# A new written order for the instructions of a fused attention and feed-forward kernel

## The chip, the cores and the metric

The kernel runs on one core of a Trainium2 chip. Its time is the device time of one execution in microseconds (us); three runs gave 105.85, 105.78 and 106.14, median 105.85. A core has TensorE (PE, matrix products, with the loading of their weights shown apart as PEld), VectorE (DVE), ScalarE (ACT), GpSimd (POOL) and SyncE (SP). SP here only issues DMAs; ACT issues a few as well. Each of them takes its instructions strictly in the order in which the program gives them, so an instruction that waits holds up all that are behind it on the same engine, DMA issues included.

## The reference

There are 4 batches and 4 heads, 1088 positions and 32 values a head. First comes an attention without softmax. `a` and `b` are 8 sketches each of q or of k, and their 64 products are the features:

```python
    def phi(x):
        a = np.einsum('rd,bhsd->bhsr', S1, x)
        b = np.einsum('rd,bhsd->bhsr', S2, x)
        return np.einsum('bhsi,bhsj->bhsij', a, b).reshape(*x.shape[:-1], r * r)
    q_p, k_p = (phi(q), phi(k))
    kv = np.einsum('bhsf,bhsd->bhfd', k_p, v)
    z = np.sum(k_p, axis=2)
    num = np.einsum('bhsf,bhfd->bhsd', q_p, kv)
    den = np.einsum('bhsf,bhf->bhs', q_p, z)[..., None] + 1e-06
```

num / den, with the heads side by side, is the 128-wide input x of a feed-forward block:

```python
    mu = np.mean(x, axis=-1, keepdims=True)
    var = np.mean((x - mu) ** 2, axis=-1, keepdims=True)
    xn = (x - mu) / np.sqrt(var + 1e-06) * g_ln
    ch = np.maximum(xn @ w_ch1, 0.0) @ w_ch2
    return (x + ch).astype(np.float32)
```

w_ch1 is 128 x 512 and w_ch2 is 512 x 128. S1, S2, w_ch1 and w_ch2 come as 64-bit floats; everything else is 32-bit.

## The kernel before

The kernel is one long list of small named steps, the text `PROGRAM`. A loop reads it from front to back and calls the function of each name; the order of the names is the order of the instructions on every engine, and dependencies between tiles become waits. Nothing reorders it. A step names its batch, its part, and where one is given its engine (S for SP, A for ACT, G for POOL, V for DVE) and its PSUM bank (X, Y, M, N, O or K).

The steps, in the order in which one batch needs them:

- Loads: `ld`, `ld_u` (k and q), `ld_vh`, `ld_v`, `ld_vr` (v), `ld_w` (the two weights), `ld_s`. `gate` is a one-column memset by POOL in the tile that a load will fill, so that the load, and every DMA behind it on SP, waits until POOL has come to that place.
- The sketch matrix: `w_bits`, `w_ex`, `w_exf`, `w_mant`, `w_e2`, `w_addlow`, `w_e3` and `s_heads` make a 32-bit S from the 64-bit words; `sk` and `sk_s` are products that turn it; `sk_0`, `sk_2`, `sk_8`, `sk_d`, `sk_q`, `sk_qq` arrange it. The two weights go the same way with `w_low`, `w_exn`, `w_en`, `w_add`, `w_mul` (the first one in two halves, columns 0 to 256 and 256 to 512); `fold` puts the layer norm's scale and centring into the first, and `fold_cp` copies it out of PSUM.
- k: `turn_u`, `turn_g`, `turn_r` transpose (DVE), `k_dir` or `k_feat` are the sketch products, `k_cp` or `k_tok` take them out of PSUM, `k_prod` forms the features (POOL, in batch 0 partly DVE as `k_prod0`), `k_sum`, `k_zs`, `k_sc`, `k_sccp` make the normaliser, `k_val` is features times v. From batch 1 on its result goes through DRAM (`k_turn`, `k_wr`, `k_rd`); in batch 0 it stays on the chip (`k_vcp`, `k_spr`, `k_rcp`).
- q: the same with `q_dir`, `q_c`, `q_dirw`, `q_ctok`, `q_cpw`, `q_ac0`, `q_den`, `q_rec`, `q_b0`, `q_prod0`, `q_turn` in batch 0, and `q_feat`, `q_tok`, `q_ac`, `q_den`, `q_rec`, `q_a2`, `q_prod`, `q_turn` later. `num` is the product of the turned q features with the k result and `num_cp` its copy: a batch gives two chunks of 512 columns (chunks 2b and 2b+1), and the remaining 64 positions of two batches form the small chunks 8 and 9.
- The feed-forward block by chunk: `hid` (one of 4 groups of 128 hidden rows, columns in quarters t0 to t1) and `relu` out of PSUM; `sec` (4 accumulating products for one quarter of the columns); `row_turn`, `row_wr`, `row_rd` bring the chunk into rows through DRAM; `st_bn`, `st_ag`, `st_pow` make the layer norm's factor; `fin` joins the parts and `store` writes out.

`fill` and `tick` compute nothing that is used: products of a tile of ones, which keep TensorE at work; `fill 8 64 O` is 8 products 64 columns wide into bank O, and `tick` is a 4-column product on a 32 x 32 corner. Every 32-bit product is carried out as two passes, so a count of 18 in the trace is 9 products.

The lines of the profile that the prediction uses: L275 is `fill`, L280 `tick`, L408 `sk`, L412 `sk_s`, L416 `sk_0`, L423 `sk_2`, L466 `turn_u`, L509 `k_dir` and `q_dir`, L556 `k_sum`, L588 `k_val`, L654 `q_ctok`, L740 `q_turn`, L756 `num`, L858 `hid`, L874 `sec`, L887 `fin`, L107 `gate`, L174 the load of the second weight, L80 ACT's copies.

Three places set the order of the work around the change. Batch 0 has nothing before it: its steps wait for loads and for each other, with DVE nearly full. From about 20 us `hid` and `sec` of one batch are laid between the attention products of the next. And in the last 20 us only `hid`, `sec`, `fin` and stores of the last chunks are left.

## Time and profile before

| | |
|---|---|
| median of 3 runs | 105.85 us |
| profiled execution, and its span | 105.92 us, 104.2 us |
| first and last TensorE product, start and end | 1.44 us, 100.45 us |
| TensorE idle from 8.48 to 43.63 us | 2.12 us |
| TensorE idle from 43.63 to 100.45 us | 0.02 us |
| first load of k landed, first load of q landed | 4.6 us, 7.1 us |
| DVE busy from 8.48 to 24.00 us | 14.00 of 15.52 us |
| POOL busy from 24.00 to 43.63 us | 16.53 of 19.63 us |

Times within the trace count from the start of the span. The span is 1.72 us shorter than the execution's own time. An engine's share of the whole span says little here: which engine ends a wait last is read for each stage.

### The profile page before, as it was taken

Reading aid. Unit: us, or ns where it says so; the run is one execution under the profiler, and the core shown is the slowest. Engines: PE = TensorE matmul, PEld = TensorE weight load, DVE = VectorE, ACT = ScalarE, POOL = GpSimd, SP = SyncE. Lnnn points to the kernel's source line nnn. Section 1 sums busy time; section 2 is a strip of 40 time slices with the busy share of each in tenths; the row PEclk is TensorE's granted clock in tenths of the full one; section 3 lists DMA queues with packets and bytes.
Section 4 is the critical chain, followed back from the end, with each engine's and each line's share of the span. In section 5 each row is a group of like instructions: output and inputs, shape, how many; then the busy total and the mean of one; then the engine's idle time right before and its main releaser. Section 6 shows DMA issues by size and latency. Waiting matters only on the chain.

```text
span 104.2 us, 3418 instructions
## 1 busy us (share of the span) xinstructions
PE 96.9 (93%) x1369; PEld 72.2 (69%) x1369; DVE 74.1 (71%) x233; ACT 36.4 (35%) x90; POOL 50.2 (48%) x69
## 2 busy tenths in 40 slices
PE   4999987999999879999999999999999999999950
PEld 4999976785545679863249779573498864499940
DVE  5619589999989599377999849986957660265530
ACT  0400628369384100053635052206620427730300
POOL 6400582543795999740299992314990300021500
PEclk9999999999999999999999999999999999999999
DMA  1898800399589467524624443423344165440442
GB/s 21 241 307 216 266 15 3 118 352 298 153 271 243 97 165 231 168 79 136 205 65 142 128 105 107 144 84 89 89 120 132 50 227 140 139 131 6 104 124 56
DMA packets 17744, 15.01 MB, mean 144 GB/s; under 512 B 5568, under 2 KB 14656, under 8 KB 17728
## 3 DMA queue, kind: packets, MB, share of 16 engines
q1 hardware_dynamic: 16240, 13.90, 45.5%
q10 hardware_dynamic: 1456, 0.89, 3.3%
q8 instruction: 11, 0.18, 0.8%
q14 instruction: 5, 0.04, 0.1%
q0 software_dynamic: 32, 0.00, 0.0%
HBM read 10.29 MB, written 4.49 MB: 142 GB/s over the span
## 4 chain that ended last, share of the span: by engine, by line
PE 92%; ACT 2%; issue 1%; DVE 1%; DVEq 0%
PE M L858 21%; PE M L874 20%; PE PO L858 9%; PE PO L874 7%; PE X L756 7%; PE PO L275 6%; PE KV L588 4%; PE X L509 3%; PE X L693 2%; PE PO L280 2%; PE X L532 2%; PE X L874 2%; PE KV L556 1%; PE KV L874 1%; PE M L509 1%
## 5 line engine op out<-in xcount | busy, mean ns | idle before, releaser
L847 POOL TENSOR_TENSOR rstd<-va,mhalf 128x4 f32<-128x4 f32 (+1 forms) x10 | 9.2, 922 | 29.5 <-DVE va L841 29.4
L874 PE MATMUL M<-w,hT 128*128 128x128 f32 x184 | 23.0, 277 | 0.0
L874 PEld LDWEIGHTS M<-w,hT 128*128 128x128 f32 x184 | 21.8, 192 | 1.6 <-ACT hT L866 0.8
L858 PE MATMUL M<-xT,w 128*128 128x512 f32 (+1 forms) x50 | 22.7, 564 | 0.0
L866 ACT ACTIVATE hT<-M 128x512 f32<-128x512 f32 (+2 forms) x29 | 14.7, 509 | 19.3 <-PE M L858 17.8
L85 POOL TENSOR_TENSOR kp<-kf 128x1024 f32<-128x1024 f32 (+3 forms) x8 | 15.0, 1890 | 1.2 <-DVE kf L541 0.6
L858 PEld LDWEIGHTS M<-xT,w 128*128 128x128 f32 x50 | 8.2, 189 | 9.0 <-issue 5.2
L85 POOL TENSOR_TENSOR qp<-a,fq 128x1280 f32<-128x1280 f32 (+1 forms) x6 | 13.0, 2175 | 0.2
L740 DVE STREAM_TRANSPOSE qpT<-qp 128x1280 f32<-128x1280 f32 (+2 forms) x9 | 11.0, 1228 | 1.6 <-POOL qp L85 1.5
L80 ACT COPY xT<-X 128x256 f32<-128x256 f32 (+1 forms) x18 | 5.6, 362 | 17.5 <-PE X L756 17.5
L866 ACT ACTIVATE hT<-PO 128x512 f32<-128x512 f32 (+2 forms) x15 | 7.3, 484 | 12.0 <-PE PO L858 11.9
L858 PE MATMUL PO<-xT,w 128*128 128x512 f32 (+1 forms) x22 | 10.6, 561 | 0.0
L834 DVE BATCH_NORM_STATS2 st<-x 128x6 f32<-128x128 f32 x32 | 6.9, 278 | 3.4 <-DMA x<-xd 2.9
L874 PE MATMUL PO<-w,hT 128*128 128x128 f32 x64 | 8.1, 278 | 0.9 <-issue 0.9
L874 PEld LDWEIGHTS PO<-w,hT 128*128 128x128 f32 x64 | 7.7, 192 | 1.8 <-issue 1.8
L756 PE MATMUL X<-qpT,kvr 32*32 32x288 f32 (+2 forms) x384 | 7.7, 332 | 0.9 <-ACT low L335 0.9
L887 DVE SCALAR_TENSOR_TENSOR ob<-M,rstd,x 128x128 f32<-128x128 f32 x21 | 6.2, 335 | 2.2 <-issue 1.1
L817 DVE STREAM_TRANSPOSE xh<-xT 128x512 f32<-128x512 f32 x8 | 5.6, 698 | 2.4 <-ACT xT L80 2.4
L756 PEld LDWEIGHTS X<-qpT,kvr 32*32 32x32 f32 x384 | 4.6, 103 | 2.9 <-ACT low L335 1.1
L275 PE MATMUL PO<-ones 128*128 128x64 f32 (+2 forms) x24 | 6.4, 430 | 0.0
L358 POOL TENSOR_TENSOR mant<-mant,low 128x256 f32<-128x256 f32 (+1 forms) x3 | 3.0, 1002 | 5.4 <-ACT mant L327 3.0
L858 PEld LDWEIGHTS PO<-xT,w 128*128 128x128 f32 x22 | 3.8, 190 | 2.4 <-issue 1.9
(132 smaller groups left out, 134.7 us busy)
## 6 DMA issues: line engine op xcount, KB each, us to landing
xd<-xh SPq DMA_DIRECT2D x8, 256.0 KB, 2.1
x<-xd SPq DMA_DIRECT2D x32, 64.0 KB, 2.0
vn<-in_v_dram SPq DMA_DIRECT2D x13, 128.0 KB, 4.1
kn<-in_k_dram SPq DMA_DIRECT2D x3, 544.0 KB, 6.0
qn<-in_q_dram SPq DMA_DIRECT2D x3, 544.0 KB, 4.5
out_dram<-ob SPq DMA_DIRECT2D x24, 64.0 KB, 1.7
qn<-in_q_dram SPq DMA_DIRECT2D x2, 256.0 KB, 4.3
w_raw<-in_moe_w_ch_dram SPq DMA_DIRECT2D x2, 256.0 KB, 4.7
```

Source lines behind the costliest of these rows:

```text
L80: act.copy(o, i)
L85: by[eng].tensor_tensor(out=o, in0=a, in1=b, op=ALU.mult)
L275: pe.matmul(banks[z][:, 0:w], ones[:, 0:P], ones[:, 0:w], start=True, stop=True)
L740: dve.transpose(_ap(qpT, 0, P, 32 * u0, [[32, u1 - u0], [TW, 8], [1, 32]]), qp[:, H * F * u0 : H * F * u1])
L756: pe.matmul(XS[r // 2][D * h : D * h + D, o : o + w], kvr[b % 2][rows, fs * f + hs * h : fs * f + hs * h + D], qpT[rows, c : c + w], start ...
L817: dve.transpose(_ap(xh[c % 2], 0, P, 0, [[32, n], [D * n, 4], [1, 32]]), cols(c))
L834: dve.bn_stats(out=sts[slot(c)][:, 6 * t : 6 * t + 6], in_=row_ap(c, t))
L847: pool.tensor_tensor(out=rstds[slot(c)][:, 0:n], in0=vas[slot(c)][:, 0:n], in1=mhalf[:, 0:n], op=ALU.pow)
L858: pe.matmul(banks[z][:, 0:n], w1[:, P * j : P * (j + 1)], cols(c)[:, a : a + n], start=True, stop=True)
L866: act.activation(o, i, AF.Relu)
L874: pe.matmul(banks[z][:, DM * t : DM * (t + 1)], h[:, 512 * j + P * t : 512 * j + P * (t + 1)], w2[:, DM * j : DM * (j + 1)], start=(j == 0 ...
L887: dve.scalar_tensor_tensor(out=o, in0=i0, scalar=rstds[slot(c)][:, t : t + 1], in1=row_ap(c, t), op0=ALU.mult, op1=ALU.add)
```

## The change

The list `PROGRAM` is replaced; no function changes. All steps that compute something stay, and the sizes of the products stay; what differs:

- The products of ones. Before: 12 and 5 small ones (`tick`), 8 of 64 columns, one of 256 behind `sk`, one of 128 behind `k_sum`, and two of 256 between the first `num` and the first `fold`. After: one of 512 and one of 368 columns ahead of `sk`, then 128 and 240 ahead of `q_c`, 240 and 256 ahead of the first `fold`, 272 behind the first `num`, 160 ahead of the first `hid`.
- Gates. Before: the second weight and k of batch 2. After: k of batch 1, the second weight, and q of batch 1.
- The orders of all engines, from the start (`c_m8`, `c_m32`, `c_m2` and the POOL memsets change places; `sk_s` comes before `k_dir`) to the end (which chunk's group goes to which bank, and when; `c_act`, a one-element activation, becomes the last step).

```diff
@@ -922,92 +922,91 @@
     PROGRAM = """
-    ld_s S 0; c_ones; ld_s A 1; c_iota; ld_u S k 0 0 4; ld_u A k 0 4 8; ld_g; c_m8; tick 12 O;
-    ld_u S q 0 0 4; ld A k 0 32 34; c_m32; fill 8 64 O; ld_w S 1 0 256; c_vpad 1; ld_vr A 0 32;
-    c_sf; w_bits V 0 0 32; w_ex V 0 0 32; ld_vh S 0; c_ident; w_exf V 0 0 32; ld_vr A 0 33;
-    c_small; w_mant V 0 0 32; w_e2 V 0 0 32; w_addlow V 0 0 32; w_e3 V 0 0 32; c_rest; s_heads V;
-    tick 5 O; c_pads 0; ld_vh S 1; sk; turn_u k 0 0 4; c_ac 0; fill 1 256 O; ld_vh S 2; sk_0;
-    turn_u k 0 4 8; k_dir 0 4 X; ld_vh S 3; turn_r k 0; c_m2; ld_u S q 0 4 8; ld S q 0 32 34;
-    w_ex V 1 0 256; w_bits V 1 0 256; k_dir 4 9 Y; turn_u q 0 0 4; ld_w S 1 256 512; k_cp A 0 4 X;
-    sk_q; w_mant A 1 0 256; ld S k 1 0 34; k_prod0 0 3 X 0; sk_8; c_cg G; k_prod G 0 3 4; sk_s;
-    k_cp A 4 9 Y; q_dir 0 4 M; sk_2; w_exn A 1 0 256; k_prod0 4 6 Y 4; k_prod G 0 6 9;
-    w_en A 1 0 256; k_sum 0; fill 1 128 O; k_zs 0; k_sc 0; w_e3 V 1 0 256; sk_qq 2; k_sccp A 0;
-    c_pads 1; turn_u q 0 4 8; q_c 0 4 X; c_vpad 0; sk_d; k_val 0; q_ctok 0 4 X; k_scd G;
-    q_ac0 0 4 M 0 0; turn_r q 0; q_den 0 0 4; w_ex V 1 256 512; q_dirw 4 9 N; q_rec 0 0 4;
-    k_vcp A 0; w_bits V 1 256 512; q_b0 0 4 M 0 0; w_exn A 1 256 512; q_prod0 0 2 M 0 0;
-    w_low A 1 0 256; w_mant A 1 256 512; k_spr 0; w_add G 1 0 256; q_turn 0 2; q_cpw A 4 9 N;
-    k_rcp A 0; q_ac0 4 9 N 4 1; w_low A 1 256 512; gate w 2; num 0 0 2; ld_w S 2 0 512;
-    q_prod0 2 4 M 0 0; w_add G 1 256 512; ld S q 1 0 34; q_den 0 4 9; fill 1 256 O; q_turn 2 4;
-    num_cp A 0 1 0 2; w_mul G 1 0 256; w_en A 1 256 512; fill 1 256 O; q_rec 0 4 9;
-    num_cp A 0 0 0 2; q_b0 4 9 N 4 1; fold O 0 256; w_e3 V 1 256 512; q_prod0 4 9 N 4 1;
-    num 0 2 4; w_mul G 1 256 512; fold_cp A O 0 256; hid M 0 0 0 2; gate k 2; c_vpad 3;
-    ld S k 2 0 34; num_cp A 0 1 2 4; c_ac 1; c_vpad 2; turn_r k 1; fold O 256 512; ld_v S 1 0;
-    sk_qq 3; q_turn 4 9; relu A M 0 0 0 2; hid N 0 1 0 2; num_cp A 0 0 2 4; ld_v S 1 1;
-    fold_cp A O 256 512; hid M 0 0 2 4; w_low A 2 0 512; ld_v S 1 2; hid O 0 2 0 2;
-    relu A M 0 0 2 4; w_bits V 2 0 512; num 0 4 9; relu A N 0 1 0 2; turn_g k 1 0 4;
-    relu A O 0 2 0 2; w_mant A 2 0 512; hid N 0 1 2 4; w_ex V 2 0 512; num_cp A 0 0 4 8;
-    num_r A 0; w_add G 2 0 512; num_cp A 0 1 4 8; k_feat 1; relu A N 0 1 2 4; row_turn 1;
-    hid M 1 1 0 4; k_tok 1; row_wr S 1; ld_v S 1 3; turn_g q 1 0 4; hid O 0 3 0 2; k_prod G 1 5 9;
-    ld_vr S 1 33; k_sum 1; relu A O 0 3 0 2; hid N 0 3 2 4; ld S q 2 0 34; w_exn A 2 0 512;
-    k_zs 1; k_sc 1; hid O 1 2 0 4; relu A N 0 3 2 4; k_sccp V 1; turn_r q 1; w_en A 2 0 512;
...
-    store S 4 0; row_rd S 7 1; sec M 6 0; st_bn 6; store S 5 2; store_r S 8 3; sec M 6 1; st_ag 6;
-    relu A N 9 1 0 1; relu A O 7 0 0 4; store_r S 8 0; st_pow 6; sec M 6 3; st_bn 7; sec M 6 2;
-    sec K 7 3; fin M 6 0; fin M 6 2; fin M 6 1; hid O 9 2 0 1; st_ag 7; sec Y 7 1;
-    relu A O 9 2 0 1; store A 4 3; fin M 6 3; st_pow 7; store S 6 0; store A 5 1; hid N 9 0 0 1;
-    sec M 7 2; store S 6 2; relu A N 9 0 0 1; st_pow 9; fin K 7 3; hid O 9 3 0 1; sec X 7 0;
-    fin M 7 2; relu A O 9 3 0 1; fin Y 7 1; store A 6 1; store A 6 3; sec N 9 0; fin X 7 0;
-    store S 7 2; store A 7 3; store S 7 0; store A 7 1; fin N 9 0; store_r S 9 0; store_r A 9 1;
-    store_r S 9 2; store_r A 9 3;
+    ld_s S 0; c_ones; ld_s A 1; c_iota; ld_u S k 0 0 4; ld_u A k 0 4 8; ld_g; c_m32; fill 1 512 O;
+    ld_u S q 0 0 4; ld A k 0 32 34; c_m2; ld_w S 1 0 256; c_vpad 1; ld_vr A 0 32; c_pads 0;
+    w_bits V 0 0 32; ld_vh S 0; c_small; c_ac 0; ld_vr A 0 33; w_ex V 0 0 32; w_mant V 0 0 32;
+    c_sf; w_exf V 0 0 32; c_ident; w_e2 V 0 0 32; w_addlow V 0 0 32; fill 1 368 O; w_e3 V 0 0 32;
+    c_m8; c_vpad 2; s_heads V; ld_vh S 1; c_rest; turn_u k 0 0 4; sk; ld_vh S 2; sk_q; sk_0;
+    turn_u k 0 4 8; sk_s; k_dir 0 4 X; ld_vh S 3; c_cg G; turn_r k 0; sk_d; turn_u q 0 0 4;
+    ld_u S q 0 4 8; k_dir 4 9 Y; k_cp A 0 4 X; ld S q 0 32 34; w_bits V 1 0 256; w_low A 1 0 256;
+    k_prod G 0 3 4; k_prod0 0 3 X 0; ld_w S 1 256 512; q_dir 0 4 M; k_cp A 4 9 Y; w_ex V 1 0 256;
+    sk_2; k_prod G 0 6 9; w_exn A 1 0 256; k_prod0 4 6 Y 4; k_sum 0; w_en A 1 0 256; k_zs 0;
+    k_sc 0; w_mant A 1 0 256; fill 1 128 O; k_sccp A 0; fill 1 240 O; c_pads 1; w_e3 V 1 0 256;
+    turn_u q 0 4 8; c_vpad 0; q_c 0 4 X; k_scd G; k_val 0; gate k 1; c_ac 1; ld S k 1 0 34;
+    q_ctok 0 4 X; w_add G 1 0 256; turn_r q 0; q_ac0 0 4 M 0 0; q_den 0 0 4; q_dirw 4 9 N;
+    w_ex V 1 256 512; k_vcp A 0; q_rec 0 0 4; w_low A 1 256 512; q_b0 0 4 M 0 0;
+    w_bits V 1 256 512; q_prod0 0 2 M 0 0; k_spr 0; q_prod0 2 4 M 0 0; fill 1 240 O;
+    q_cpw A 4 9 N; w_exn A 1 256 512; gate w 2; w_mul G 1 0 256; fill 1 256 O; ld_w S 2 0 512;
+    q_ac0 4 9 N 4 1; w_mant A 1 256 512; q_turn 0 2; w_en A 1 256 512; w_add G 1 256 512;
+    fold O 0 256; k_rcp A 0; q_den 0 4 9; q_rec 0 4 9; num 0 0 2; w_e3 V 1 256 512;
+    q_b0 4 9 N 4 1; w_mul G 1 256 512; q_turn 2 4; fill 1 272 M; num_cp A 0 1 0 2;
+    fold_cp A O 0 256; q_prod0 4 9 N 4 1; fold M 256 512; num_cp A 0 0 0 2; fill 1 160 O;
+    fold_cp A M 256 512; hid O 0 1 0 2; gate q 1; sk_8; num 0 2 4; ld S q 1 0 34; q_turn 4 9;
+    w_low A 2 0 512; ld S k 2 0 34; hid M 0 2 0 2; ld_v S 1 0; num_cp A 0 1 2 4; num_cp A 0 0 2 4;
+    hid N 0 3 0 2; ld_v S 1 1; w_bits V 2 0 512; num 0 4 9; ld_v S 1 2; w_ex V 2 0 512;
+    relu A N 0 3 0 2; turn_r k 1; relu A O 0 1 0 2; ld_v S 1 3; turn_g k 1 0 4; w_mant A 2 0 512;
+    hid N 0 3 2 4; num_cp A 0 0 4 8; w_add G 2 0 512; num_r A 0; hid O 0 0 2 4; num_cp A 0 1 4 8;
+    relu A N 0 3 2 4; k_feat 1; row_turn 1; relu A M 0 2 0 2; relu A O 0 0 2 4; hid M 0 0 0 2;
+    row_wr S 1; k_tok 1; hid O 0 1 2 4; ld_vr S 1 33; relu A M 0 0 0 2; turn_g q 1 0 4;
+    k_prod G 1 5 9; k_sum 1; ld S q 2 0 34; hid N 1 2 0 4; k_zs 1; turn_r q 1; turn_r k 2; k_sc 1;
+    hid M 0 2 2 4; k_sccp V 1; turn_g k 2 0 4; q_feat 1; k_prod G 1 0 5; relu A M 0 2 2 4;
+    relu A N 1 2 0 4; hid M 1 0 0 4; w_exn A 2 0 512; q_tok 1 1; q_tok 1 0; hid N 1 3 0 4;
+    w_en A 2 0 512; relu A O 0 1 2 4; sk_qq 2; w_e3 V 2 0 512; k_val 1; relu A N 1 3 0 4;
+    row_rd S 1 1; q_ac V 1 4 9; q_ac V 1 0 4; ld S k 3 0 34; w_mul G 2 0 512; q_den 1 4 9;
...
+    relu A N 7 0 0 4; row_rd S 6 2; st_bn 9; hid O 9 1 0 1; st_ag 9; row_rd S 7 3;
+    relu A M 7 2 0 4; sec N 6 0; row_rd S 7 1; row_rd S 7 0; hid M 9 0 0 1; relu A O 9 1 0 1;
+    sec N 6 2; relu A M 9 0 0 1; row_rd S 7 2; store A 5 1; store_r S 8 2; sec N 6 1; store S 2 2;
+    hid O 9 2 0 1; store S 4 2; st_bn 6; hid M 7 1 0 4; relu A O 9 2 0 1; store A 5 3; sec N 6 3;
+    st_ag 6; relu A M 7 1 0 4; st_bn 7; st_pow 6; sec Y 7 1; st_ag 7; sec X 7 0; fin N 6 2;
+    st_pow 9; fin N 6 0; sec M 7 2; st_pow 7; fin N 6 1; fin N 6 3; store S 6 0; store A 6 1;
+    hid O 9 3 0 1; fin X 7 0; sec K 7 3; store S 6 2; relu A O 9 3 0 1; fin Y 7 1; store A 4 1;
+    fin M 7 2; store A 6 3; sec N 9 0; fin K 7 3; store S 7 0; store A 7 3; store A 7 1;
+    store S 7 2; fin N 9 0; store_r A 9 3; store_r S 9 0; store_r S 9 2; store_r A 9 1; c_act;
     """
```

## The prediction

> **What bounds the kernel now.** First the page's first two parts: how full each engine is, and where.

> ```profile
> span 104.2 us, 3418 instructions
> PE 96.9 (93%) x1369; PEld 72.2 (69%) x1369; DVE 74.1 (71%) x233; ACT 36.4 (35%) x90; POOL 50.2 (48%) x69
> ...
> PE   4999987999999879999999999999999999999950
> ...
> DVE  5619589999989599377999849986957660265530
> ```

> TensorE is full nearly everywhere, so the end is its start plus its work plus its pauses. Which part of that work is useful shows in the chain that ended last, in order of time (start, length, what):

> ```profile
> 1.44 1.44 PE PO L280 x24
> 2.88 3.60 PE PO L275 x16
> 6.48 0.62 PE PO L280 x10
> 7.11 0.72 PE KV L408 x2
> 7.83 0.85 PE PO L275 x2
> 8.68 3.53 PE X L509 x18
> ...
> 36.14 0.92 issue
> ...
> 99.54 0.91 PE M L874 x8
> ```

> The reader is to see that sk (L408) starts at 7.11 behind 5.7 us of products of ones, and that the 18 passes of k_dir (L509) take 196 ns each. Third, the instructions in order of time, DVE's of the start:

> ```profile
> 3.63 0.28 DVE L85 TENSOR_TENSOR s_f<-mant,bits 16x128 f32<-16x128 f32 x1
> 4.61 1.09 DVE L466 STREAM_TRANSPOSE kT<-kn 128x512 f32<-128x512 f32 x1 [0.70 <-DMA kn<-in_k_dram]
> 7.87 0.23 DVE L416 TENSOR_TENSOR sk<-KV,m 128x64 f32<-128x64 f32 x1 [2.16 <-PE KV L408]
> 10.83 0.96 DVE L85 TENSOR_TENSOR kp<-X,kf 128x768 f32<-128x768 f32 x1 [0.38 <-ACT kf L80]
> 12.47 0.29 DVE L423 TENSOR_TENSOR s2b<-KV,m 128x128 f32<-128x128 f32 x1 [0.69 <-PE KV L412]
> 13.68 0.19 DVE L564 TENSOR_TENSOR zT<-KV,m 128x32 f32<-128x32 f32 x1 [0.28 <-PE KV L556]
> 15.10 0.32 DVE L654 STREAM_TRANSPOSE qc<-X 128x128 f32<-128x128 f32 x1
> 22.38 1.47 DVE L740 STREAM_TRANSPOSE qpT<-qp 128x1280 f32<-128x1280 f32 x1
> ```

> sk's operand (the first row) is ready at 3.91; DVE loses 2.16 us to sk all the same. From there to 24 us DVE is busy 14.00 of 15.52 us: it sets the pace of batch 0. From 43.63 to 100.45 TensorE never pauses. Fourth, products by group, 11.0 to 11.5 us and then 12.3 to 13.4 us:

> ```profile
> L509 PE MATMUL X<-sk,kT 128*128 128x128 f32 x5 | 1.3, 420 | 0.0
> ```
> ```profile
> L509 PE MATMUL M<-sk,qT 128*128 128x128 f32 x8 | 1.1, 275 | 0.0
> ```

> The same product takes 420 ns, then 275: TensorE runs at half rate until about 11.7 us, though the granted clock reads 1.00 throughout.

> **The change, part by part.** The sum is made against the profiled execution, 105.92 us (span 104.2, 1.72 around it); the median is 0.07 lower.

> *Products of ones at the start.* 12 + 5 small ones and 8 of 64 columns go. At half rate a 128-column pass takes 0.196 us, so 512 and 368 columns, two passes each, take 2 x (4.0 + 2.88) x 0.196 = 2.7 us: from 1.44 to 4.1, some 0.2 later with the first weights. Then sk can start at about 4.4: c_m8 (0.10 and 0.16) now stands ahead of s_heads, which then ends near 4.3. sk takes 0.72, so sk_0 waits only for turn_u, which no order can start before k's landing at 4.6: it runs at 5.70, not 7.87. That is 2.17 us. k_dir follows at 6.0 (before 8.48).

> *DVE up to q_ctok.* The waits of 0.38, 0.69 and 0.28 us in the rows above go: k_cp and sk_s are earlier, and k_sum is ready when k_zs comes. c_m2, 0.25 by the spacing of its rows, moves ahead of k's landing, into DVE's 0.70 of waiting. Next late are the loads, whose issues up to the first weight's second half stand in the old order: q at 7.1 (0.2 us of waiting at turn_u), then w_e3, held by ACT's conversions (0.1), and q_ctok behind the longer fill (128 + 240 columns, 0.77 us against 0.27; about 0.25 of it shows). So 2.17 + 1.35 + 0.25 - 0.55 = 3.2; I take 3.1, q_ctok at 12.0. This has k_dir at full rate, 18 x 0.111 (q_dir's 0.89 over 8). At half rate the second k_cp comes 1.3 us later and k_prod0 4 6 0.7: 2.4 instead of 3.1. Which, depends on whether 2.7 us of wide products and sk wake TensorE where 9 us of narrow ones did not before 11.7. I take full rate, because from 7 us on the products were wide and the change came 4.7 us later; both ends stay in the range. [...]

> *q_ctok to the last q_turn.* 8.75 us before; the same instructions, without turn_r k 1 (0.22), which comes right behind. So q_turn 4 9 ends at 20.75, not 23.85, and 2.9 of lead stays on DVE. The fills here: 240 + 256 columns (1.03 by the 0.53 of a 256-column one) lie between k_spr, done at 14.7, and the first num, which waits for k_rcp behind three conversions on ACT (0.5 each) until 16.4: hidden, with 0.1 to spare. 272 columns (0.56) lie in the wait for w_mul's second half; 160 (0.33) in the wait of num 0 4 9 for q_turn. Without these covers they would cost their 2.2 us; the two removed fills of 256 (1.06) lay beside DVE work as well.

> *TensorE at num 0 4 9.* It starts at 20.8, not 23.91, but three half-width hid products lie behind it, not four: 0.45 of the 3.1 is owed. The lead is 2.65.

> *Loads and gates.* Issues take 0.4 to 0.5 each on SP. k of batch 1 (544 KB, ungated at 8.77 before) now waits for a gate behind k_scd, about 11.5, and the second weight for one behind w_add, 12.4 (before 18.10). Both move where the DMA share was 0.02 (13.33 to 18.47). At the 300 GB/s of the busy slices 1.06 MB take 3.5 us: landed near 16.5, first read at 20.8. Behind gate q 1 (POOL, after the second w_mul, 17.9) SP holds q 1, k 2 and v of batch 1, 1.65 MB: 5.5 us and 2 of latency, 25.4. turn_g q 1 wants q at 24.8, which comes first (about 22); k_val 1 wants v at 29.4. Hidden; if the transfers ran at the 200 GB/s of 24 to 43 us, v would come at 28.2 and still be in time.

> *POOL.* The memsets change places while POOL waits; sk_qq 2 (0.39) moves into its full stretch, ahead of w_mul. k_prod 2 then ends near 41.3, before 43.66, and k_val 2 starts near 42: hidden.

> *From batch 1 on.* The same products in a new order. Before, TensorE's pauses from 24 to 100 were 0.92 us at 36.14, with no releaser shown. I leave it in (0 to 0.92 to gain). New waits: hid M 2 3 comes 4.3 us after num 1's start and needs bank M, which fin 1 frees; before, st_bn 1 to the last fin took 3.86 and began 0.2 behind num's start, so 0.2 us of room. Likewise hid N 6 1 behind fin 4, room 0.25, and the last k_rd 3, ten issues behind the stores that follow k_wr 3, room 1.5. I take 0.2 of loss, with 0 and 1.5 as ends (all three rooms missed by one slow issue of 1.6, as k_rd at 38.24 was). c_act (0.2) stands behind ACT's last issue, while stores still land: nothing. The end, one sec, one fin and four small stores, is as before: 3.75 us.

> Sum: 105.92 - 2.65 + 0.2 = 103.47; less 0.07 for the median, 103.4.

> **Rivals.**

> 1. *The lead is given back in part.* k_dir stays at half rate (0.7), and the three rooms are missed (1.3): 103.4 + 0.7 + 0.6 to 1.3, about 104.9. For it: POOL is busy 16.53 of 19.63 us up to num 1. Against it: the pauses after 24 us were 0.92 in all.
> 2. *The head was not the bound.* If batch 1 waits for a load or POOL anyway, all is given back and it stays at 105.9. Against it: loads of batch 1 have free DMA time, and POOL's k_prod 1 starts from k_tok, which moves with DVE.
> 3. *TensorE falls back to half rate, and it is slower.* Place: from k_dir to the first num the new order has pauses (about 1 us between k_sum and k_sc). The work there, fills included, is 8.6 us at full rate, by the rows; at half rate 17.2, and the first num would start at 23.2 instead of 16.4, the lead of 2.65 turned into a loss of 3.2 with the fold and fills that lay behind it before: 109. Up to 2.65 us of lost time it is not slower, so it decides once the half rate lasts over some 5.3 us of products. Against it: pauses of 0.28 and 0.93 us from 13.3 to 18.5 (TensorE busy 3.94 of 5.14) brought none before. [...]

> **Numbers.** Forecast 0.58, own range 102.5 to 104.3; rival 1 0.15; rival 2 0.07; slower 0.20, half of it rival 3 (107 to 109) and half waits in the new order beyond the ends above, just over 106. The lowest end is the lead of 3.1 with the 0.92 gone: 101.9. Runs here differ by 0.3%, so changes below that count as none. Faster 0.73, same 0.07, slower 0.20; range 102.2 to 106.4, which leaves out some 0.05 below and 0.13 above.

> **What would show it.** sk_0 at 5.7 to 6.0; k_dir's passes at 275 ns; q_ctok at 12.0; num 0 4 9 at 20.8; TensorE without pauses of over 0.3 us from there but the one near 33 to 36, and its last product ending near 97.9. It is wrong if L509 stays at 420 ns, if hid or num wait for loads, or if TensorE pauses after 40 us.

## The result and the profile after

The changed kernel takes 104.85 us in the median of 20 executions (102.09 to 108.39); the kernel before, on the same occasions, took 106.75 in the median of 20 (105.17 to 109.38). One kernel's executions differ by up to 6%, so the ratio is formed from those within 1.5% of each kernel's fastest (4 of the changed kernel's, 10 of before's): 0.967, with a 95% interval of 0.961 to 0.973. The medians of all executions alone would give 0.982. Forecast were 103.4 us against 105.85, a ratio of 0.977.

The profiled execution of the changed kernel took 104.31 us (span 102.5, 1.81 around it). Its page, first two parts:

```profile
span 102.5 us, 3333 instructions
PE 95.9 (94%) x1327; PEld 69.1 (67%) x1327; DVE 73.3 (71%) x233; ACT 36.6 (36%) x90; POOL 50.0 (49%) x70
...
PE   4979898999999999999999999999999999999950
...
DVE  4995589997998789369975996679459790237720
```

TensorE's row has no gap left in its middle: the 0.92 us at 36.14 of before is gone. The last product ends at 98.77 (before 100.45), and from there to the end of the span it is 3.7 us in both, so all of the gain lies ahead of the last product. DVE's rows of the start, from the instructions in order of time (start, length, what; in brackets the wait and what ended it):

```profile
4.11 0.27 DVE L85 TENSOR_TENSOR s_f<-mant,bits 16x128 f32<-16x128 f32 x1
4.54 1.08 DVE L466 STREAM_TRANSPOSE kT<-kn 128x512 f32<-128x512 f32 x1 [0.16 <-DMA kn<-in_k_dram]
5.54 0.23 DVE L416 TENSOR_TENSOR sk<-KV,m 128x64 f32<-128x64 f32 x1
8.82 0.96 DVE L85 TENSOR_TENSOR kp<-X,kf 128x768 f32<-128x768 f32 x1 [1.07 <-ACT kf L80]
11.01 0.69 DVE L85 TENSOR_TENSOR kp<-X,kf 128x512 f32<-128x512 f32 x1 [0.83 <-ACT kf L80]
12.09 0.19 DVE L564 TENSOR_TENSOR zT<-KV,m 128x32 f32<-128x32 f32 x1 [0.39 <-PE KV L556]
13.88 0.32 DVE L654 STREAM_TRANSPOSE qc<-X 128x128 f32<-128x128 f32 x1 [0.41 <-PE X L646]
20.86 1.51 DVE L740 STREAM_TRANSPOSE qpT<-qp 128x1280 f32<-128x1280 f32 x1
```

sk_0 (L416) runs at 5.54 and no longer waits: 2.33 us earlier than before. But the waits for ACT's copies (L80) have grown to 1.07 and 0.83, and q_ctok (L654) comes at 13.88, only 1.22 earlier. TensorE's products show why; the first block is from its instructions in order of time from 5 to 7 us, those in the second block its groups from 5.5 to 11 us (busy, mean ns of one, idle before):

```profile
5.91 0.77 PE L412 MATMUL KV<-s_f,ident 128*128 128x128 f32 x2 [0.61 <-DVE sk L416]
6.46 0.85 PE L509 MATMUL X<-sk,kT 128*128 128x128 f32 x3
```
```profile
L509 PE MATMUL X<-sk,kT 128*128 128x128 f32 x18 | 4.0, 421 | 0.0
L509 PE MATMUL M<-sk,qT 128*128 128x128 f32 x4 | 1.0, 402 | 0.0
```

All 18 passes of k_dir ran at half rate, 421 ns each instead of 275. And sk_s (L412), which the new order puts ahead of k_dir, waited 0.61 us for sk_0, which reads the PSUM tile of the same name, KV; k_dir came behind it, at 6.46. From q_ctok on the trace adds up: the lead is 15.10 - 13.88 = 1.22 at q_ctok and 23.91 - 22.71 = 1.20 at num 0 4 9; the extra hid behind it takes back 0.45, the vanished pause gives 0.92, which makes 1.67; the last product shows 1.68. So in this execution the vanished pause is more than half of the gain.

**When full rate begins.** Half rate is here the name for the state in which a pass of k_dir takes 421 ns and all 18 take 4.0 us; in full rate they take 275 ns and 2.2 us (experiment 1). That the first is exactly half of the second these numbers do not show. Beside the instructions the trace has a record of changes of the clock. It does not show the half rate at the start, but it has an entry where the passes of L509 (k_dir, then q_dir) get short: in before they take 420 ns up to 11.5 us and 275 from 12.0 on, with the entry at 11.75; in the changed kernel 421 up to 10.5 and 275 from 11.5 on, with the entry at 11.08:

```
kernel and profiled execution   full rate, by the record   length
before             105.92 us    11.75 to 103.91 us         92.16 = 27 x 3.413
changed            104.31 us    11.08 to 103.24 us         92.16 = 27 x 3.413
```

In experiment 2 below, full rate lasts from 5.09 to 42.64, 11 x 3.413, and a half rate behind it one such length, to 46.05. Where the start of full rate is given below, the mean clocks of the other traced executions agree with 27 or 28 lengths: in old_gates full rate begins at 6.37, 27 lengths end at 98.53, and half rate from there to the end of the span at 100.2 makes 0.992, which it has. In these traces the changes of the rate thus lie on a raster of 3.413 us, and its place against the kernel's start differs between executions: full rate began at 11.08 in this execution of the changed kernel and at 5.04 in that of experiment 1. The windows of the changed kernel along the raster (length; busy PE, PEld, DVE, ACT, POOL; granted clock; DMA share; GB/s):

```profile
0.85:4.26 3.41, 2.81 (x4) 1.18 (x4) 2.89 (x19) 0.94 (x1) 2.65 (x16) 1.00 0.52 142
4.26:7.67 3.41, 2.79 (x11) 2.30 (x11) 3.24 (x8) 0.52 (x2) 0.63 (x2) 1.00 0.97 283
7.67:11.08 3.41, 3.41 (x18) 3.41 (x17) 1.51 (x5) 1.24 (x4) 0.65 (x2) 1.00 0.78 221
```

The first interval began before TensorE's first product, at 1.45, the second holds the wait of sk_s; the third is the first that TensorE filled, and full rate begins at its end.

### The profile page after: what moved, and what is told of

Read it like the earlier page. It is cut to its first block, busy times and chain, and to the rows that moved or that the text cites. A ratio compares the mean times of both kernels' runs of the same rounds, so it can differ in the third digit from the quotient of the medians.

```text
span 102.5 us, 3333 instructions
## 1 busy us (share of the span) xinstructions
PE 95.9 (94%) x1327; PEld 69.1 (67%) x1327; DVE 73.3 (71%) x233; ACT 36.6 (36%) x90; POOL 50.0 (49%) x70
## 4 chain that ended last, share of the span: by engine, by line
PE 84%; DVE 6%; DMA 5%; POOL 1%; issue 1%; SPq 0%; ACTq 0%; ACT 0%; POOLq 0%
PE M L874 23%; PE M L858 20%; PE PO L858 11%; PE X L756 6%; PE X L509 4%; PE PO L874 3%; PE KV L588 3%; DMA kn<-in_k_dram 3%; PE X L693 2%; PE X L532 2%; PE X L874 2%; DMA out_dram<-ob 2%; PE KV L556 1%; PE M L509 1%; DVE qp L85 1%; DVE kT L466 1%
## 5 line engine op out<-in xcount | busy, mean ns | idle before, releaser
L874 PEld LDWEIGHTS M<-w,hT 128*128 128x128 f32 x216 | 25.5, 192 | 2.9 <-issue 2.1
L874 PE MATMUL M<-w,hT 128*128 128x128 f32 x216 | 26.9, 277 | 0.0
L858 PE MATMUL M<-xT,w 128*128 128x512 f32 (+1 forms) x46 | 21.4, 566 | 0.0
L866 ACT ACTIVATE hT<-M 128x512 f32<-128x512 f32 (+2 forms) x28 | 13.8, 505 | 13.4 <-PE M L858 13.2
L85 POOL TENSOR_TENSOR kp<-kf 128x1024 f32<-128x1024 f32 (+3 forms) x8 | 15.0, 1889 | 5.2 <-ACT kf L80 4.1
L740 DVE STREAM_TRANSPOSE qpT<-qp 128x1280 f32<-128x1280 f32 (+2 forms) x9 | 11.1, 1235 | 4.5 <-POOL qp L85 4.5
L866 ACT ACTIVATE hT<-PO 128x512 f32<-128x512 f32 (+2 forms) x16 | 8.0, 499 | 15.6 <-PE PO L858 15.5
L85 POOL TENSOR_TENSOR qp<-a,fq 128x1280 f32<-128x1280 f32 (+1 forms) x6 | 13.0, 2174 | 0.5
L858 PE MATMUL PO<-xT,w 128*128 128x512 f32 (+1 forms) x26 | 12.4, 558 | 0.0
L80 ACT COPY xT<-X 128x256 f32<-128x256 f32 (+1 forms) x18 | 5.5, 365 | 11.0 <-PE X L756 11.0
L756 PE MATMUL X<-qpT,kvr 32*32 32x288 f32 (+2 forms) x384 | 7.7, 332 | 0.4 <-ACT kvr L80 0.4
L887 DVE SCALAR_TENSOR_TENSOR ob<-M,rstd,x 128x128 f32<-128x128 f32 x25 | 7.1, 342 | 0.8 <-PE M L874 0.3
L275 PE MATMUL PO<-ones 128*128 128x240 f32 (+5 forms) x14 | 5.6, 527 | 1.4 <-DVE bit L237 1.4
L756 PEld LDWEIGHTS X<-qpT,kvr 32*32 32x32 f32 x384 | 4.6, 103 | 2.6 <-ACT kvr L80 0.8
L588 PEld LDWEIGHTS KV<-kp,vn 128*32 128x32 f32 x288 | 4.3, 110 | 1.7 <-issue 0.9
L702 DVE STREAM_TRANSPOSE fq<-X 128x576 f32<-128x576 f32 x6 | 4.5, 756 | 0.8 <-PE X L693 0.8
```

Of the source, the lines that this page charges most:

```text
L85: by[eng].tensor_tensor(out=o, in0=a, in1=b, op=ALU.mult)
L275: pe.matmul(banks[z][:, 0:w], ones[:, 0:P], ones[:, 0:w], start=True, stop=True)
L588: pe.matmul(KV[D * h : D * h + D, 0:F], vn[b][:, TW * h + D * u : TW * h + D * (u + 1)], kp[:, H * F * u + F * h : H * F * u + F * (h + 1) ...
L740: dve.transpose(_ap(qpT, 0, P, 32 * u0, [[32, u1 - u0], [TW, 8], [1, 32]]), qp[:, H * F * u0 : H * F * u1])
L756: pe.matmul(XS[r // 2][D * h : D * h + D, o : o + w], kvr[b % 2][rows, fs * f + hs * h : fs * f + hs * h + D], qpT[rows, c : c + w], start ...
L858: pe.matmul(banks[z][:, 0:n], w1[:, P * j : P * (j + 1)], cols(c)[:, a : a + n], start=True, stop=True)
```

## The experiments

**The theory**: full rate begins at the first boundary of the raster behind an interval that TensorE fills with wide products. The changed kernel's products run without a gap from 1.45 to about 5.3 us only, so the interval fits in if a boundary falls between 4.9 and 5.3; otherwise full rate waits for the interval behind the gap, 9.3 to 12.7. **The rivals**: the wide products do little, and the new order behind them (fills, gates, places of loads) makes the gain; or what differs between executions is when loads land. Each kernel ran in six executions (the last one in seven), beside the kernel before, whose median was 106.48, 106.26 and 106.66 us in the three sessions.

**1. The changed kernel again, unedited** (after_again).

> The changed kernel once more, nothing edited. Two theories. Raster theory: TensorE goes to full rate only at the ticks of a fixed raster of 3.41 us whose place differs from execution to execution, and only after a whole interval without a pause; the order of the change has one pause of 0.62 us at 5.3 us (before sk_s), so either a tick falls between 4.9 and 5.3 (about one execution in seven) and k_dir runs at full rate, 275 ns a product, with a time near 102.1, or it comes between 9.3 and 12.7 and the time is 103.7 to 105. Then in this profile k_dir's rate and the time go together: 275 ns with 102 to 103, or 420 ns with 104 and more. Rival, memory theory: the spread between executions comes from when the loads land; then k_dir stays at 420 ns in a profile near 102 too, and q_ctok or turn_u start earlier because their load landed earlier than 4.51 (k) or 6.61 us (q).

Measured: median 103.51 (102.32 to 108.48), ratio 0.972 (0.966 to 0.978). This profiled execution took 102.32 us, with full rate from 5.04, the end of an interval (1.63 to 5.04) with TensorE busy for all of its 3.41 us. Its groups from 5.5 to 11 us:

```profile
L509 PE MATMUL X<-sk,kT 128*128 128x128 f32 x18 | 2.2, 275 | 0.0
L509 PE MATMUL M<-sk,qT 128*128 128x128 f32 x8 | 1.1, 275 | 0.0
```

Same program, k_dir now at 275 ns: q_ctok comes at 11.59 instead of 13.88 and the last product ends at 96.79 instead of 98.77. So in this pair of executions the rate moves the end by 2.0 us, with a new loss of 0.39 already taken off. That loss, in this execution's instructions in order of time:

```profile
40.08 1.34 PE L756 MATMUL X<-qpT,kvr 32*32 32x288 f32 x47 [0.39 <-DMA kvr<-kvd]
```

num of batch 1 (L756) waits for kvr, the k result read back by k_rd 1. In the execution of 104.31 us the four reads of it landed between 40.63 and 42.06, just as num 1 began at 41.99: there was no room to spare.

**2. The gap closed by a fill** (gap_filled).

```diff
-    turn_u k 0 0 4; sk; ld_vh S 2; sk_q; sk_0;
+    turn_u k 0 0 4; sk; fill 1 256 O; ld_vh S 2; sk_q; sk_0;
```

> One more product of ones, 256 columns wide, between sk and sk_s, so that TensorE has no pause from 1.45 us on. Raster theory: every execution has a whole busy interval by 8.3 us at the latest, so part or all of k_dir and all of q_dir run at full rate in every execution, k_dir ends near 8.6 to 9.5 (10.51 before), and nearly all executions fall near the fast ones of the changed kernel: 102 to 103.3, median some 2 us below the changed kernel's. Rival (loads, or a fixed delay of about 11 us since the start): k_dir stays at 420 ns until 11 us, and the added 0.85 us of products makes it 0.2 to 0.3 us slower.

Measured: median 104.63 (102.62 to 106.75), ratio 0.978 (0.970 to 0.986): no better than the changed kernel. (The kernel before has such a fill behind sk; the change had taken it out.) The profiled execution took 105.47 us although full rate began at 5.09 and q_ctok came at 11.4. Its instructions in order of time, and the windows along its raster (columns as above):

```profile
36.74 2.84 PE L874 MATMUL M<-w,hT 128*128 128x128 f32 x24
41.59 2.11 PE L756 MATMUL X<-qpT,kvr 32*32 32x288 f32 x64 [2.00 <-DMA kvr<-kvd]
```
```profile
35.81:39.22 3.41, 3.41 (x33) 3.41 (x33) 2.90 (x5) 0.00 (x0) 3.41 (x3) 1.00 0.80 215
39.22:42.64 3.42, 1.42 (x57) 1.03 (x66) 0.32 (x2) 0.00 (x0) 1.14 (x1) 1.00 0.31 110
42.64:46.05 3.41, 3.41 (x104) 2.33 (x80) 1.20 (x10) 1.32 (x5) 1.05 (x1) 0.50 0.28 79
46.05:49.46 3.41, 3.41 (x38) 1.01 (x37) 3.22 (x10) 1.19 (x2) 0.00 (x0) 1.00 0.33 107
```

num 1 waited 2.00 us. The interval with that wait had TensorE busy for 1.42 of 3.42 us, and the next one ran at half rate (granted clock 0.50; the 72 passes of k_val in it took 2.15 us, 1.21 in the execution of 104.31): lost are the 2.00 us and half of 3.41. One such interval makes a mean clock of 1 - 0.5 x 3.41 / 103.7 = 0.984, which this execution has. The wait's cause is among its DMA issues from 34 to 39.2 us (KB each, us from issue to landing):

```profile
qn<-in_q_dram SPq DMA_DIRECT2D x1, 544.0 KB, 6.6
...
kvr<-kvd SPq DMA_DIRECT2D x4, 32.0 KB, 5.9
```

The four reads of 32 KB stand on SP right behind q of batch 3, 544 KB, which nothing needs yet, and land only 5.9 us after their issue (4.1 and 4.7 in the two executions of the changed kernel). They stand there in the kernel before too: its load of q 3 was issued at 37.71, the third read landed at 42.73, and num 1 began at 43.63 without a wait. The theory of the raster was right for the head and missed the time; a second place that costs had been found.

**3. sk_s put back behind k_dir** (sk_s_later): k_dir no longer stands behind the wait for sk_0.

```diff
-    turn_u k 0 4 8; sk_s; k_dir 0 4 X;
+    turn_u k 0 4 8; k_dir 0 4 X;
-    k_dir 4 9 Y; k_cp A 0 4 X;
+    k_dir 4 9 Y; sk_s; k_cp A 0 4 X;
```

> sk_s back behind k_dir, where the kernel before has it; nothing else. In the profile sk_s starts at 5.91, after sk_0, and k_dir only behind it at 6.46. If sk_s waits for sk_0 because both use the same PSUM bank, k_dir starts 0.5 us earlier, near 5.9 to 6.0, at half rate ends near 10.0, and the time falls by 0.3 to 0.5 us in like executions. Rival: sk_s is hidden behind another wait of k_dir (turn_u), k_dir still starts at 6.4, no change.

Measured: median 104.6 (104.36 to 107.41), ratio 0.989 (0.984 to 0.993). In the profiled execution (104.71) k_dir starts at 5.95 instead of 6.46 and q_ctok comes at 13.33 instead of 13.88, with full rate from 9.86; num 1 waits 0.62 us for kvr. That does not show the order of sk_s to be worth anything at half rate: full rate also came 1.22 us earlier here than at 11.08. The profile of experiment 7 has sk_s in front of k_dir and full rate from 9.55, and there q_ctok comes at 13.15, no later than 13.33. What k_dir gains DVE pays again: sk_2 waits 0.71 us for the later sk_s, which it does not do in the changed kernel.

**4. The small products of before at the start** (narrow_start).

```diff
-    fill 1 512 O;
+    tick 12 O; fill 8 64 O;
-    fill 1 368 O;
+    tick 5 O;
```

> The changed kernel with the start products of the kernel before (12 and 5 small ones, 8 of 64 columns) in place of the two wide ones; everything else as changed. If the earlier start is the gain: sk at 7.1 instead of 4.54, sk_0 at 7.7, k_dir near 8.4, and 2.0 to 2.5 us slower than the changed kernel in like executions, so within 1 us of the kernel before. Rival: the new orders after the start make the gain, and the start is worth under 0.8 us.

Measured: median 107.13 (106.5 to 108.27), ratio 1.012 (1.006 to 1.017): about 1% slower than before. In its profiled execution (107.27) sk_0 comes at 8.08, full rate at 13.31, q_ctok at 16.27. TensorE was busy from 3.07 to 6.48 without a gap, with these narrow products, and the rate did not rise; it rose at the end of 9.90 to 13.31, the first filled interval behind sk_s's wait. With the small products at the start the new order is a loss.

**5. Only the wide products, in the kernel before** (wide_in_before).

```diff
-    c_m8; tick 12 O;
+    c_m8; fill 1 512 O;
-    fill 8 64 O;
-    tick 5 O;
+    fill 1 368 O;
```

> One part alone: the kernel before, with only its start products exchanged for one of 512 and one of 368 columns (its product of 256 behind sk stays and covers the pause there). If the start is the gain: sk at 4.4, sk_0 at 5.6, k_dir near 6.0 and at full rate at the latest from 8.3 on, num 1 some 2.2 to 3 us earlier than before, unless a load holds it, and 103 to 104 against 105.9 in like executions. Rival (the new orders make the gain): 105.3 or more.

Measured: median 103.57 (102.83 to 104.29), ratio 0.986 (0.978 to 0.993). Profiled execution 103.5: full rate from 5.14, sk_0 at 5.39, k_dir at 5.66 (sk_s stands behind it here), q_ctok at 11.7. The last product ends at 98.0, 2.45 us ahead of before; with full rate from the same time the new order ended it at 96.79. TensorE's pauses from 14 us on were 1.87 us here, 0.97 of them one wait of the first num for ACT, and 0.99 in the new order's execution: that is 0.9 of the 1.2. The old order has a wait for the reads of k_rd 1 as well, 0.23 us, once its num 1 comes earlier. By medians this exchange alone does as much as the whole change: 2.7 us below before's of its session, the changed kernel 1.9 and 3.0.

**6. Without the six later fills** (no_later_fills): of 128, 240, 240, 256, 272 and 160 columns.

```diff
-    fill 1 128 O; k_sccp A 0; fill 1 240 O;
+    k_sccp A 0;
...
-    q_prod0 2 4 M 0 0; fill 1 240 O;
+    q_prod0 2 4 M 0 0;
-    fill 1 256 O; ld_w S 2 0 512;
+    ld_w S 2 0 512;
-    fill 1 272 M; num_cp A 0 1 0 2;
+    num_cp A 0 1 0 2;
-    fill 1 160 O;
```

> The changed kernel without its six later products of ones (128, 240, 240, 256, 272 and 160 columns, 2.7 us of TensorE); the two wide ones at the start stay. If they only lie in waits, as the prediction had it, num 0 4 9 starts within 0.2 us of where it did in like executions and the time stays, as long as the rate does. If the pauses that they fill are long enough for the half rate to come back, the trace shows an interval of 3.41 us at half rate between 9 and 20 us and the time grows by 0.5 to 1.7. Rival: they delay q_c and the first hid, and without them it is 0.3 to 0.6 faster.

Measured: 102.29, 106.88, 105.41, 102.42, 104.83 and 106.75 us; ratio 0.974 (0.964 to 0.985). The profiled execution, the first, had full rate from 5.38: its first num came at 15.53 (15.61 in after_again) and its last product ended at 96.7 (96.79). The fills take no time, as forecast. Without them TensorE paused 1.59 us at 13.94 and 0.75 at 16.37; its windows along the raster, columns as above:

```profile
12.21:15.62 3.41, 1.82 (x30) 1.45 (x35) 3.36 (x10) 2.32 (x7) 1.01 (x2) 1.00 0.85 282
15.62:19.03 3.41, 2.66 (x133) 1.99 (x132) 3.36 (x6) 1.66 (x5) 0.96 (x3) 1.00 0.35 97
```

An interval with 1.82 busy of 3.41 did not lower the rate here. But three of the six executions, without a trace, had mean clocks of 0.944, 0.977 and 0.967 and took 105.41 to 106.88. The lowest of the changed kernel's was 0.968, so the fills seem to keep the rate up rather than cost anything; without a trace of such an execution that is argued, not shown.

**7. q of batch 3 loaded behind k_rd 1** (k_rd_first).

```diff
-    ld_vr S 2 33; ld S q 3 0 34;
+    ld_vr S 2 33;
-    row_rd S 1 0;
+    row_rd S 1 0; ld S q 3 0 34;
```

> The changed kernel with one load moved: q of batch 3 (544 KB) is issued on SP behind the reads of batch 1's k result (k_rd) and rows instead of ahead of them; it is read only ten microseconds later. In the traces so far num 1 waits 0.39, 0.62 and 2.00 us for those reads, which land just behind that load, and after the pause of 2.00 TensorE ran at half rate for 3.41 us. Queue theory: k_rd 1 lands some 4 us earlier, near 36 to 38, num 1 starts without a pause behind its sec, the drop to half rate near 42 is gone, and the spread narrows: the slow end (105.5 to 108.5) goes, times 102 to 105 by the phase of the start alone; median 0.5 to 1.5 us below the changed kernel's. Rival (the landing of k_rd is late through the v loads or the DRAM round trip, not through q 3): num 1 still pauses by 0.4 us or more, and the executions of 105 to 108 stay.

Measured: median 102.89 (101.89 to 104.61), ratio 0.971 (0.963 to 0.978); all six mean clocks 0.999 or more, where the changed kernel had executions between 0.968 and 0.984. The reads in its DMA issues from 33 to 39 us:

```profile
kvr<-kvd SPq DMA_DIRECT2D x4, 32.0 KB, 3.0
```

3.0 us instead of the 5.9, 4.7 and 4.1 above, and num 1 does not wait. This profiled execution (103.72) had full rate from 9.55, as the gap at the start leaves open, and the times that remain are those of the start: three near 102, three at 103.7 to 104.6. Three of six is more than the one in seven expected in experiment 1; with so few executions the share is left open.

**8. Both: the gap closed and the reads first** (gap_and_k_rd, and again in another session as gap_and_k_rd_again).

> Both edits: the product of ones that fills the pause behind sk, and q 3 behind k_rd 1. If the start's raster and the queue behind q 3 are the two sources of the spread, nearly all executions lie within 102.0 to 103.5, the median 2 to 4 us below the kernel before, and it beats the changed kernel. Rival: a third source; executions of 105 and more are as frequent as in the changed kernel.

> The best version so far once more, beside the others on one chip: six of six executions between 102.0 and 104.0 if the two sources of the spread (pause in the start's interval, k_rd 1 behind q 3) were all; any execution over 105 shows a third.

Measured: median 102.8 (102.27 to 103.72), ratio 0.980 (0.972 to 0.988); again 102.36 (101.81 to 102.62), ratio 0.967 (0.961 to 0.972). The last session's page, chain in order of time and TensorE at num 1:

```profile
span 100.6 us, 3338 instructions
```
```profile
1.45 3.30 PE PO L275 x4
4.75 0.55 PE KV L408 x2
5.30 0.85 PE PO L275 x2
6.15 0.53 PE KV L412 x2
6.68 1.19 PE X L509 x8
```
```profile
37.77 2.40 PE L874 MATMUL M<-w,hT 128*128 128x128 f32 x20
40.09 1.60 PE L756 MATMUL X<-qpT,kvr 32*32 32x288 f32 x64
```

From 1.45 on TensorE has no gap, so by the length of an interval one is filled by 1.45 + 2 x 3.41 = 8.3 us at the latest: full rate came at 6.74 in the one profile and 7.15 in the other, and num 1 follows the product ahead of it without a wait. The fastest is hardly faster than the changed kernel's luckiest executions (102.09), but all twelve lie between 101.81 and 103.72. The changed kernel's median in the first session was 103.51; the two medians here, set against before's of their sessions, stand 3.5 and 4.3 us below it, the changed kernel's 3.0 (and 1.9 on the occasions of the result).

**9. The same with sk_s behind k_dir** (gap_k_rd_sk_s; the edits of 3 and 8 together).

> The best version so far (pause behind sk filled, q 3 behind k_rd 1) with sk_s back behind k_dir. In the trace of that version sk_s runs at 5.9 behind sk_0 and k_dir begins at 6.57. If sk_s costs its place: k_dir begins near 5.9 to 6.0, q_ctok 0.3 to 0.5 earlier (near 11.5 against 11.87), times 101.8 to 103.2 and the median 0.2 to 0.5 below that version's 102.8. Rival: DVE's turn_u sets k_dir's second half anyway and q_ctok stays at 11.8, no change.

Measured: median 102.7 (102.29 to 105.49), ratio 0.970 (0.964 to 0.975). In the profiled execution k_dir starts at 5.94 rather than 6.47, but q_ctok at 11.85 rather than 12.01, and the last product ends at 96.71 rather than 96.80: with full rate, too, the order of sk_s is worth nothing at the end. The one execution of 105.49 (mean clock 0.984) has no trace; it is open where it lost an interval.

**10. The same as 8 with the gates of before** (old_gates): k and q of batch 1 ungated and as early as before, k of batch 2 gated.

```diff
-    ld_w S 1 256 512; q_dir 0 4 M;
+    ld_w S 1 256 512; ld S k 1 0 34; q_dir 0 4 M;
-    gate k 1; c_ac 1; ld S k 1 0 34;
+    c_ac 1;
-    ld_w S 2 0 512;
+    ld_w S 2 0 512; ld S q 1 0 34;
-    gate q 1; sk_8; num 0 2 4; ld S q 1 0 34; q_turn 4 9;
+    gate k 2; sk_8; num 0 2 4; q_turn 4 9;
```

> The best version so far with the gates of the kernel before: k of batch 1 loaded without a gate behind the first weight's second half, q of batch 1 right behind the second weight, a gate ahead of k of batch 2. The prediction costed the gates at nothing. If that holds, median and range stay within 0.4 us of that version's. Rival (loading apart is worth something): loads of the first weight's second half or of q land later through k 1, or turn_g q 1 or k_feat 1 wait, and it is 0.5 us or more slower.

Measured: median 101.95 (101.73 to 102.65), ratio 0.965 (0.959 to 0.971), beside 102.36 and 0.967 for 8 in the same session; profiled execution 101.97, q_ctok at 11.64, num 1 at 39.69, last product 96.39. The new gates gain nothing; if they cost, it is 0.4 us, within what the intervals leave open. Old gates with the rest is the fastest median of all.

**11. No products at the start** (no_start; kernel 7 without the two wide ones).

```diff
-    fill 1 512 O;
-    fill 1 368 O;
```

> The version with only q 3 moved, without the two wide products at the start: nothing runs on TensorE before sk at 4.4. sk, sk_0 and k_dir begin where they did (4.4, 5.55, 6.47). Raster theory: the first whole busy interval lies behind 6 us, so no execution has k_dir at full rate from its start; full rate comes between 9.4 and 12.8, no time near 102, all six at 103.5 to 105.5. Rival (the wide products do not matter for the rate, it comes by itself): as many executions near 102 as with them (3 of 6).

Measured: median 103.86 (103.52 to 104.66), ratio 0.980 (0.975 to 0.985), none near 102. In the profiled execution (104.66) the first product, sk, ran at 4.53 and k_dir from 6.61 to 10.65; its groups from 5.5 to 11 us:

```profile
L509 PE MATMUL X<-sk,kT 128*128 128x128 f32 x18 | 4.0, 421 | 0.0
```

sk_0 is nearly as early without the wide products as with them (5.70 against 5.55 in experiment 7). So two things were in their exchange: the small ones had delayed sk by 2.5 us, which taking them out cures, and the wide ones can raise the rate before k_dir, which saves the other 2 us when an interval fits.

## Why the prediction was right, and where its sum was off

The forecast mechanism held: the head was the bound, sk came earlier, and what was gained there lasted to the end. The ratio of 0.967 lies a point beyond the forecast 0.977, that of all medians half a point short of it, and the two traced executions lie on both sides of the forecast: last product at 97.9, measured 98.77 and 96.79. That the forecast lies between them is in part luck, since it took one rate for all executions and its errors offset each other. At full rate the gain was 3.51 of lead - 0.45 + 0.92 - 0.39 = 3.59, at half rate 1.22 - 0.45 + 0.92 = 1.69; forecast 2.65 - 0.2 = 2.45. One of the prediction's own signs of being wrong, L509 at 420 ns, came in the execution of 104.31 us.

- **Products at the start**: right. sk at 4.4 forecast, 4.54 and 4.55 measured; sk_0 5.70 forecast, 5.54 and 5.50. Experiments 4, 5 and 11 show it to be the cause.
- **k_dir at 6.0**: missed by 0.15 at full rate and 0.46 at half. The step had sk_s as nothing but an instruction that is earlier; what it did not count is that the moved sk_s waits for sk_0 (0.61 us) and k_dir stands behind it (6.46, and 5.95 with sk_s put back).
- **"I take full rate"**: this is the step that failed as put; it was the author's estimate from one trace, that of before. It is neither yes nor no: it depends on where the raster lies, half rate in one traced execution, full in the other. The term was also mis-sized. The prediction gave 2.4 of lead at half rate, 0.7 less than 3.1; measured are 1.22 (q_ctok 13.88) and 3.51 (11.59). The price of half rate is 2.3, because k_cp and k_prod0 do not hide it: the first k_prod0 came 1.13 later (8.82 against 7.69), the second 2.05 (11.01 against 8.96), and k_zs 2.49 (12.09 against 9.60). At full rate the lead was 0.4 better than the 3.1.
- **0.45 owed behind num 0 4 9**: right, by the sum shown with the result. **The pause of 0.92**, left in with 0 to 0.92 to gain: it went, the upper end. It is absent from wide_in_before too, which keeps the old order there, so that the new order removed it is not shown. In before's trace the pause ends at 37.07, as an instruction transfer of 8 KB (queue q14, from 36.59) does; whether TensorE waited for that, no run settles.
- **Later fills hidden**: right in time (experiment 6). **Gates and loads, POOL, c_act hidden**: right; c_act ran at 100.35 while SP's last wait for stores ended at 101.39, and the end took 3.74, forecast 3.75.
- **Rooms**: the 0.2 taken for hid M 2 3 and hid N 6 1 did not appear. The room that was missed was another: the prediction named the last k_rd, k_rd 3, ten issues behind stores, and not k_rd 1, which stands right behind q of batch 3 in both kernels and had at most 0.9 us of room before (third read landed at 42.73, num 1 at 43.63). Of the profiles that keep this order those of before and of the execution of 104.31 us show no wait; wide_in_before, after_again and sk_s_later lost 0.23, 0.39 and 0.62 us and gap_filled 2.00, there with 1.7 more through the rate.
- **Rival 1** (lead given back in part, 104.9): half of it happened, half rate in k_dir without the missed rooms; the profiled 104.31 lies below its 104.9. **Rival 3** (half rate comes back): that short pauses bring it back was the author's assumption; the trace of before has full rate from 11.75 to 103.91, its pauses included. Its place, from k_dir to the first num, had no fall in either traced execution of the changed kernel, though experiment 6 had low clocks in three executions when the fills there were taken out. A fall behind a pause occurred elsewhere, at num 1 in gap_filled (2.00 us), and at a smaller price: one interval, 1.7 us, not the 8.6 of a whole stretch. By the mean clocks (0.968 to 0.984) five of the changed kernel's 20 executions lost such an interval or two and took 105.49 to 108.39 us; they have no trace, so that theirs was the wait at num 1 is argued from experiments 2 and 7, not shown. The kernel before has such executions too, with mean clocks of 0.983 and 0.984 and 108.4 to 109.8 us in the three sessions.

## What to carry to other kernels

Where TensorE sets the pace, ask of every start and every wait not only how long it is but what rate the products behind it have: here a gap of 0.61 us in the first 8 us went with 421 ns a pass instead of 275 and cost 2.0 us in one of two traced executions of the same program, and one small fill in it, together with the reads put ahead of the load, made the time steady (twelve executions between 101.81 and 103.72 us). At the start, prefer wide products to narrow ones (medians of 103.51 and 107.13 in one session), and let nothing narrow stand ahead of the first useful one (sk_0 at 5.54 and 8.08). And when a stage is to come earlier, look at what stands ahead of each small read that it waits for in the DMA queue: the room of 0.9 us that was enough before was not enough then, with waits of 0.39, 0.62 and 2.00 us in experiments 1, 3 and 2.
